# Attention backward: second half of dS transposed by DMA in eleven of fifteen steps of a head group instead of seven

## The chip, the cores and the metric

The kernel runs on one core of a Trainium2 chip. The metric is the device time of one execution in microseconds (us). The core has TensorE (PE; its weight loads are listed apart as PEld), VectorE (DVE), ScalarE (ACT), GpSimd (POOL), SyncE (SP), which here only issues DMAs, and 16 DMA engines that work through what SP and ACT issue. Each engine has its instructions in an order fixed by the program; between engines they wait on semaphores.

## The reference

The model is four layers on x of 2048 x 640: a linear attention (A), a sliding window attention (B), and both again with the same weights. The kernel computes the output and the gradients of the input and of the four weight matrices (`jax.vjp`). What the change touches is the backward of layer B, whose forward is, for 32 heads of width 20 and a causal window of 256:

```python
scores = jnp.einsum("bhqd,bhkd->bhqk", q, k) * (Dh ** -0.5)
mask = (idx[:, None] - idx[None, :] >= 0) & (idx[:, None] - idx[None, :] < W)
p = _softmax(jnp.where(mask[None, None], scores, -1e9), axis=-1)
o = jnp.einsum("bhqk,bhkd->bhqd", p, v)
```

Its backward needs, for each block of 128 queries and 128 keys inside the window, E = exp(scores), the product dP of the output's gradient with V, dS = dP * E, and from these dQ = dS K, dK = dS' Q and dV = E' dO (the softmax's sums and the row term of its backward are worked into dO and into the padding of each head from 20 to 32 columns beforehand). In the kernel scores and dS lie with the keys on the partitions. dK and dV can use them as they are; dQ needs dS turned, 128 x 128 block by block.

## The kernel before

The order of the program is: `forward` (all four layers, with what the backward needs saved to DRAM), `B_attn_bwd` for layer 3, a phase `bwd_phase` of dense work (weight gradients, layer norms, the linear attention of layer 2), `B_attn_bwd` for layer 1, and a last `bwd_phase`.

`B_attn_bwd` is a loop written out by hand: the order in which it calls the engines is the order of the program on each of them (`tc.manual_schedule`). The first loads of `bwd_phase`, though, stand on SP's queue between the last DMAs of `B_attn_bwd`.

The 32 heads are taken in G = 8 groups of four. A group has NB = 15 steps; a step n (0 to NS - 1 = 119) covers one block of 128 queries (t = n % 15 + 1) against its three key blocks (`blocks`). A step has two halves, h = 2n + p, of two heads each: p = 0 is the first head pair and p = 1 the second. For each half the loop does, in this order:

- `dve_ds(h)`, line 1575: VectorE multiplies dP (in PSUM, tile `pair`) by E into `ds_sb`.
- `mm_s(h + 3)` and `mm_dp(h + 2)`, line 1540: TensorE computes the scores of a half that comes three halves later (K and Q) and dP of one that comes two halves later (V and dO). Both write `pair`, of which PSUM holds three: the scores of a half go where the dS of three halves ago was read, and dP goes over the scores of its own half once the exponential has read them.
- `act_exp(h + 3)`, line 1560: ScalarE's exponential from `pair` to `e_sb`; GpSimd masks two of its blocks (lines 1564 and 1567).
- `turn(h)`, from line 1578: dS of the half is transposed, either by six matmuls with the identity into the one PSUM tile `dsT_ps` (line 1588), or, where the condition in line 1581 holds, by one DMA transpose on SP's queue from `ds_sb` straight to `dsT` in SBUF (`dma_t`, line 326).
- `copy_t`, line 1592: what lies in `dsT_ps` is copied to `dsT`: on ScalarE for first halves, on VectorE for second halves, the latter in the first half of the next step. Where `turn` used the DMA there is nothing to copy.
- `evac`, line 1613: VectorE moves a finished accumulator `dqvk_ps` to `dqkv`, once a step.
- `mm_acc`, lines 1604 and 1608: TensorE accumulates dQ, dK and dV of the block whose own step was three steps ago, two heads in each half; its dQ part reads the `dsT` of that step. In step 2 of a group two blocks are done, all four heads of the last block of the group before in the first half, and the first block of this group in the second.

PSUM is full: three `pair` of two banks, `dsT_ps`, and `dqvk_ps`. `dsT` has eight buffers, one for each half, `ds_sb` five and `e_sb` seven, one for each step.

At the start of steps 0, 2, 4, ... 12 one load of the next group's slabs is put on SP: first Q, K, V and dO by DMA transposes out of DRAM, then K, Q and dO plain. In the last group the weights of the next phase (`wq`) are loaded in their place. So all DMAs of this loop are issued by SP, in the order in which the loop comes to them.

Of the kernel before, what the change touches and what calls it, by code (L numbers as in the profile page):

```python
# [200 lines left out]
class Kern:  # L201
# [1298 lines left out]
    def B_attn_bwd(self, l, dqkv, slab0=None, first=None):  # L1500
        nc, tc, D, T, TT, H, G, DP = self.nc, self.tc, self.D, self.T, self.TT, self.H, self.G, self.DP
        ld, E, DS, PR, TPS, TSB, ACC = {}, {}, {}, {}, {}, {}, {}
        with ExitStack() as st:
# [15 lines left out]
            NB = TT - 1  # L1519
            NS = G * NB  # L1520
# [57 lines left out]
            def turn(h):  # L1578
                n, p = divmod(h, 2)
                t = TSB[h] = pe.tile([P, 2, 3, P], BF, name="dsT", bufs=8)  # L1580
                if p == 1 and n % NB % 2 == 1 and n < NS - 6:
                    self.dma_t(t.rearrange("p i j q -> p (i j) q"),
                               DS[n][:, 2 * p:2 * p + 2].rearrange("p i j q -> p (i j q)"))
                    return
                ps = TPS[h] = pps.tile([P, 2, 3, P], BF, name="dsT_ps")
                for i in range(2):
                    for j in range(3):
                        nc.tensor.transpose(ps[:, i, j, :], DS[n][:, 2 * p + i, j, :], self.ident)  # L1588
# [38 lines left out]
            with tc.manual_schedule(engines={mybir.EngineType.PE, mybir.EngineType.DVE, mybir.EngineType.SP,  # L1627
# [7 lines left out]
                for h in range(2 * (NS + 4)):  # L1635
                    n, p = divmod(h, 2)
                    here = n < NS
                    if here and not p:
                        if n % NB == 0:
                            todo = loads(n // NB + 1) if n // NB + 1 < G else next_weights()  # L1640
                        if n % NB % 2 == 0 and todo:
                            todo.pop(0)()
                    if here:
                        dve_ds(h)
                        mm_s(h + 3)
                        mm_dp(h + 2)
                        act_exp(h + 3)
                        turn(h)
                    if (h - 1) % 2:
                        copy_t(h - 1)  # L1650
                    for o in done:
                        evac(*o)
                    done = []
                    if not p:
                        copy_t(h)
                    units = outs.get(n, [])
                    if len(units) == 2:
                        units, heads = [units[p]], range(4)
                    else:
                        heads = (0, 1) if p == 0 else (2, 3)  # L1660
                    for o in units:
                        mm_acc(*o, heads)
                        if heads[-1] == 3:
                            done.append(o)
# [84 lines left out]
```

## Time and profile before

| | |
|---|---|
| median of 3 runs | 2271.16 us (2267.75 to 2272.58) |
| profiled execution | 2272.93 us, of which the span 2271.2 |
| granted TensorE clock, mean | 0.964 |
| attention backward of layer 3, all 120 steps | about 782 to 1104 us |
| attention backward of layer 1, all 120 steps | about 1548 to 1870 us |
| DMA transposes of dS in the whole run | 106 (53 in each attention backward) |

The span is the time from the first to the last instruction in the profile; the time of an execution is a little longer. "Busy" is the sum of an engine's instruction times; a matmul's time is long against the distance to the next one, since they are pipelined, so that distances between starts say more about TensorE than its busy time does. In a timeline a row gives the start, the time, the engine, the line, what is written and what is read, and the number of instructions that were merged; in brackets is idle time before it, with what ended it. A window row gives the busy time of each engine in that stretch.

### The profile page before, as it was taken

How to read it: one execution, taken by the hardware profiler on the slowest of the kernel's cores; microseconds unless marked ns; L12 is line 12 of the kernel's file. 1: busy time of each engine (PE TensorE's matmuls, PEld its weight loads, DVE VectorE, ACT ScalarE, POOL GpSimd, SP SyncE). 2: the span in 40 equal slices, each digit the busy share in tenths (PEclk: the TensorE clock that was granted, in tenths of full speed). 3: DMA queues.
4: the chain of work that ended last, by engine and by line, in shares of the span. 5: the costliest groups of instructions: out<-in, count | busy, mean ns of one | idle time of the engine just before them, and what ended most of it. 6: DMA issues, size and time to landing. Idle time of an engine off the chain costs nothing. (4 is left out here: it accounts for less than half of the span.)

```text
span 2271.2 us, 68393 instructions
## 1 busy us (share of the span) xinstructions
PE 2020.9 (89%) x28066; PEld 1415.0 (62%) x28066; DVE 1452.7 (64%) x2990; ACT 1195.5 (53%) x1981; POOL 883.0 (39%) x1850
## 2 busy tenths in 40 slices
PE   6878998869998798998799889998998988997899
PEld 4645666646666577777566567656777775665664
DVE  6656777567776389899534359606889984443551
ACT  4527777527787488888422123216888871110330
POOL 1015566416777355555222113204555541220110
PEclk9989999989999899999899999999999999998999
DMA  7469988599997576767787789845776768877964
GB/s 261 164 156 197 188 169 184 131 234 212 208 212 155 121 134 125 130 131 138 162 175 157 186 172 210 172 111 125 121 132 124 133 137 180 194 166 189 197 146 102
DMA packets 930059, 371.29 MB, mean 163 GB/s; under 512 B 810064, under 2 KB 910032, under 8 KB 929488
## 3 DMA queue, kind: packets, MB, share of 16 engines
q1 hardware_dynamic: 851968, 293.13, 63.8%
q10 hardware_dynamic: 77776, 73.79, 10.4%
q8 instruction: 219, 3.59, 0.7%
q14 instruction: 96, 0.79, 0.1%
HBM read 109.02 MB, written 112.07 MB: 97 GB/s over the span
## 5 line engine op out<-in xcount | busy, mean ns | idle before, releaser
L1575 DVE TENSOR_TENSOR ds_sb<-pair,e_sb 128x768 bf16<-128x768 f32 x480 | 436.3, 948 | 27.0 <-PE pair L1540 23.6
L1560 ACT ACTIVATE e_sb<-pair 128x768 bf16<-128x768 f32 x480 | 389.3, 812 | 116.8 <-PE pair L1540 111.2
L804 POOL TENSOR_SCALAR_AFFINE_SELECT e_sb<-e_sb 128x384 bf16<-128x384 bf16 (+1 forms) x512 | 199.7, 409 | 381.5 <-ACT e_sb L795 340.1
L795 ACT ACTIVATE e_sb<-s_ps 128x1152 bf16<-128x1152 f32 (+2 forms) x256 | 273.7, 1069 | 104.9 <-PE s_ps L791 79.1
L1058 PE MATMUL mm_ps<-wq,dqT 128*128 128x320 bf16 x1920 | 284.6, 303 | 20.5 <-DMA dqT<-dqkv 19.0
L1567 POOL TENSOR_SCALAR_AFFINE_SELECT e_sb<-e_sb 128x256 bf16<-128x256 bf16 x448 | 182.9, 408 | 267.9 <-ACT e_sb L1560 259.6
L1058 PEld LDWEIGHTS <-om 128*128 128x128 bf16 x1760 | 176.1, 100 | 165.4 <-DMA om<-o 13.0
L1229 POOL TENSOR_TENSOR gw<-w,gcar 128x640 f32<-128x640 f32 x64 | 89.5, 1398 | 477.5 <-ACT w L1226 456.7
L1058 PE MATMUL mm_ps<-dqkv,om 128*128 128x480 bf16 x1280 | 269.6, 368 | 0.0
L1058 PEld LDWEIGHTS <-dqT 128*128 128x128 bf16 x1920 | 186.4, 99 | 97.6 <-DMA dqT<-dqkv 23.2
L1564 POOL TENSOR_SCALAR_AFFINE_SELECT e_sb<-e_sb 128x256 bf16<-128x256 bf16 x512 | 207.5, 409 | 91.3 <-ACT e_sb L1560 90.0
L1211 ACT ACTIVATE dh<-mm_ps 128x320 f32<-128x320 f32 x128 | 56.0, 438 | 329.2 <-PE mm_ps L1058 279.3
L1588 PE MATMUL dsT_ps<-ident,ds_sb 128*128 128x128 bf16 x2244 | 193.3, 224 | 29.2 <-ACT dsT L1592 25.7
L1588 PEld LDWEIGHTS <-ds_sb 128*128 128x128 bf16 x2244 | 140.4, 99 | 92.5 <-issue 89.2
L1592 ACT COPY dsT<-dsT_ps 128x768 bf16<-128x768 bf16 x240 | 191.0, 796 | 11.6 <-PE dsT_ps L1588 5.3
L1604 PE MATMUL dqvk_ps<-Ksl,dsT 128*128 128x32 bf16 x2160 | 167.6, 178 | 4.8 <-DVE dqkv L1613 3.0
L1604 PEld LDWEIGHTS <-dsT 128*128 128x128 bf16 x2880 | 156.3, 97 | 24.1 <-issue 22.0
L439 PE MATMUL mm_ps<-Wqkv_B,hnTB 128*128 128x320 bf16 x960 | 169.0, 306 | 0.6 <-DVE qk_slab L683 0.3
L1608 PE MATMUL dqvk_ps<-Qsl,ds_sb 128*128 128x32 bf16 x2160 | 165.4, 177 | 0.0
L1608 PE MATMUL dqvk_ps<-dOsl,e_sb 128*128 128x32 bf16 x2160 | 165.3, 177 | 0.0
L1540 PE MATMUL pair<-KTg,QTg 32*128 32x384 bf16 (+2 forms) x768 | 122.4, 323 | 26.1 <-DVE ds_sb L1575 24.3
L1608 PEld LDWEIGHTS <-ds_sb 128*128 128x128 bf16 x2880 | 145.2, 96 | 0.0
(199 smaller groups left out, 3919.3 us busy)
## 6 DMA issues: line engine op xcount, KB each, us to landing
qkvp<-qk_slab SPq DMA_DIRECT2D x64, 256.0 KB, 3.4
hn<-hn SPq DMA_DIRECT2D x64, 160.0 KB, 2.8
om<-hn SPq DMA_DIRECT2D x20, 512.0 KB, 4.5
qkvp<-v_slab SPq DMA_DIRECT2D x32, 256.0 KB, 3.1
o<-o SPq DMA_DIRECT2D x48, 160.0 KB, 3.1
om<-o SPq DMA_DIRECT2D x15, 512.0 KB, 4.6
Ksl<-qkvp SPq DMA_DIRECT2D x12, 512.0 KB, 4.5
Qsl<-qkvp SPq DMA_DIRECT2D x12, 512.0 KB, 4.6
```

Source lines behind the costliest of these rows:

```text
L439: nc.tensor.matmul(ps.t[:, w0:w0 + width], lhsT=lhsT(), rhs=rhs(), start=start, stop=stop)
L795: op("ACT", av(3 * nkt * P), lambda: nc.scalar.activation(e.t[:, 0:3, 0:nkt, :], s3.t[:, :, 0:nkt * P].rearrange("p h (i q) -> p h i q", q=P),
L804: nc.gpsimd.affine_select(out=v, in_=v, compare_op=ALU.is_ge, fill=0.0, base=0, pattern=[[0, h1 - h0], [1, P]], channel_multiplier=-1)
L1058: nc.tensor.matmul(ps.t[:, w0:w0 + width], lhsT=lhsT(), rhs=rhs(), start=start, stop=stop)
L1560: nc.scalar.activation(e, PR[h][:, :, 0:3 * P].rearrange("p i (j q) -> p i j q", q=P), ACT.Exp, scale=self.c_att)
L1564: nc.gpsimd.affine_select(out=e[:, :, j, :], in_=e[:, :, j, :], compare_op=ALU.is_ge, fill=0.0, base=0, pattern=[[0, 2], [-1, P]], channel ...
L1567: nc.gpsimd.affine_select(out=e[:, :, j, :], in_=e[:, :, j, :], compare_op=ALU.is_ge, fill=0.0, base=-1, pattern=[[0, 2], [1, P]], channel ...
L1575: nc.vector.tensor_mul(DS[n][:, hs], PR.pop(h)[:, :, 0:3 * P].rearrange("p i (j q) -> p i j q", q=P), E[n][:, hs])
L1588: nc.tensor.transpose(ps[:, i, j, :], DS[n][:, 2 * p + i, j, :], self.ident)
L1592: (nc.vector.tensor_copy if h % 2 else nc.scalar.copy)(TSB[h], TPS.pop(h))
L1604: nc.tensor.matmul(a[:, 0, hh, :], lhsT=TSB[2 * n + hh // 2][:, hh % 2, j, :], rhs=ld[g]["K"][:, k, cs], start=(i == 0), stop=(i == len(dq ...
L1608: nc.tensor.matmul(a[:, 1 + x, hh, :], lhsT=src[n][:, hh, j, :], rhs=ld[g][rhs][:, q, cs], start=(i == 0), stop=(i == len(dkv) - 1))
```

## The change

In a head group, `turn` gives the second half of step n to the DMA when n % 15 is 1, 3, 5, 7, 9, 11 or 13 before the change, and when it is 1, 3, 5 or 7 to 14 after it. The last six steps of the run (n >= 114) use TensorE in both. Nothing else is edited.

```diff
             def turn(h):
                 n, p = divmod(h, 2)
                 t = TSB[h] = pe.tile([P, 2, 3, P], BF, name="dsT", bufs=8)
-                if p == 1 and n % NB % 2 == 1 and n < NS - 6:
+                if p == 1 and n % NB not in (0, 2, 4, 6) and n < NS - 6:
                     self.dma_t(t.rearrange("p i j q -> p (i j) q"),
                                DS[n][:, 2 * p:2 * p + 2].rearrange("p i j q -> p (i j q)"))
                     return
```

On TensorE the six matmuls and six weight loads of such a half go, on VectorE its copy; on SP one DMA transpose comes in, behind the load of that step where there is one (steps 8, 10 and 12) and ahead of the first load of the next group (step 14).

## The prediction

> **What bounds the kernel now.** First the page: its span and its busy shares.
>
> ```profile
> span 2271.2 us, 68393 instructions
> PE 2020.9 (89%) x28066; PEld 1415.0 (62%) x28066; DVE 1452.7 (64%) x2990; ACT 1195.5 (53%) x1981; POOL 883.0 (39%) x1850
> ...
> L1592 ACT COPY dsT<-dsT_ps 128x768 bf16<-128x768 bf16 x240 | 191.0, 796 | 11.6 <-PE dsT_ps L1588 5.3
> ```
>
> No engine is full over the span, and the change lies only in the two runs of the attention backward (about 782 to 1104 us and 1548 to 1870 us). There four engines work within a tenth of each other, so I went to the windows and the timeline of a stretch in the middle of a head group. I call a step D if the second half of its dS is transposed by DMA, P if by TensorE. ScalarE's copy of line 1592 runs once in each step, for the first half, and marks the steps. From copy to copy, step 6 (P) lasts from 839.57 to 842.37, and step 7 (D) to 844.85:
>
> ```profile
> 839.57:842.37 2.80, 2.57 (x70) 2.19 (x66) 2.38 (x5) 2.22 (x3) 1.54 (x4) 1.00 0.98 106
> 842.37:844.85 2.48, 2.22 (x49) 1.58 (x46) 2.36 (x4) 2.37 (x5) 1.54 (x4) 1.00 0.79 178
> 901.60:941.60 40.00, 36.02 (x808) 28.64 (x808) 36.10 (x55) 34.37 (x46) 23.06 (x60) 1.00 0.67 129
> 941.60:982.30 40.70, 36.93 (x809) 29.18 (x808) 36.23 (x55) 34.52 (x46) 23.05 (x60) 0.96 0.70 126
> ```
>
> The columns are the window, its length, busy us of PE, PEld, DVE, ACT and POOL, the granted clock, the DMA engines' busy share and GB/s. P costs 2.80, D 2.48; the third row is a whole head group, 40.0 us, the fourth one in which the clock fell once. Now what sets each. The timelines of ScalarE and of TensorE:
>
> ```profile
> 839.57 0.80 ACT L1592 COPY dsT<-dsT_ps 128x768 bf16<-128x768 bf16 x1
> 840.26 0.82 ACT L1560 ACTIVATE e_sb<-pair 128x768 bf16<-128x768 f32 x1
> 841.66 0.81 ACT L1560 ACTIVATE e_sb<-pair 128x768 bf16<-128x768 f32 x1 [0.58 <-PE pair L1540]
> 842.37 0.79 ACT L1592 COPY dsT<-dsT_ps 128x768 bf16<-128x768 bf16 x1
> 843.11 1.68 ACT L1560 ACTIVATE e_sb<-pair 128x768 bf16<-128x768 f32 x2
> 844.85 0.80 ACT L1592 COPY dsT<-dsT_ps 128x768 bf16<-128x768 bf16 x1
> ```
>
> ```profile
> 840.42 0.50 PE L1588 MATMUL dsT_ps<-ident,ds_sb 128*128 128x128 bf16 x6 [0.23 <-ACT dsT L1592]
> ...
> 841.29 0.33 PE L1540 MATMUL pair<-KTg,QTg 32*128 32x384 bf16 x2
> ...
> 841.56 0.51 PE L1588 MATMUL dsT_ps<-ident,ds_sb 128*128 128x128 bf16 x6
> ...
> 843.98 0.34 PE L1540 MATMUL pair<-VTg,dOTg 32*128 32x384 bf16 x2
> 844.25 0.51 PE L1588 MATMUL dsT_ps<-ident,ds_sb 128*128 128x128 bf16 x6
> ```
>
> In a P step the copy (839.57) must first empty the one dsT_ps buffer; then come the second half's transposes (840.42, +0.85), behind them on TensorE the accumulation and the scores of a later half (841.29, +0.87), its exponential (841.66, +0.37) and the next copy (842.37, +0.71): 2.80. In a D step that loop does not exist, and another sets the pace: copy (842.37), the next exponential behind it on ScalarE (843.11, +0.74), the dP product, which overwrites the pair that this exponential reads (843.98, +0.87), the next step's first transposes behind it (844.25, +0.27), and the next copy (844.85, +0.60): 2.48.
>
> **The change, part by part.** In a group, steps 8, 10, 12 and 14 go from P to D. The last group has only step 8 of these before n reaches 114. That is 7 x 4 + 1 = 29 in each attention backward, 58 in all.
>
> *Removed, for each:* six TensorE transposes with their weight loads (0.335 from the first start at 841.56 to the accumulation behind them), one VectorE copy out of dsT_ps (mean 557 ns by its group, 134 of them now, 76 after) and its place between two uses of dsT_ps. These are not added up as costs: they are why the loop of 2.80 vanishes. *Price:* the step falls back to the loop of 2.48, which has neither the removed transposes nor VectorE's copy in it. That is 0.32 us a conversion.
>
> No two D steps follow each other now, so what a row of them takes must be bounded. From below: ScalarE alone, at its shortest distances (copy to exponential 0.69 at 844.85, exponential to exponential 0.87, exponential to copy 0.71 at 841.66), needs 2.27; VectorE's evacuations before and behind the D step stand 2.25 apart (841.42 and 843.67). With 2.27 for all, a pair takes 4.54 against 5.28 now: 0.74 a conversion, 43 us. From above: a pair that stays at 5.28 gains nothing. I take 2.48, since the loop that shows it closes within one step (copy to next copy) and its five links stay in the same order on ScalarE and TensorE when the next step is D too; the ends that could free it, an earlier exponential or an earlier dP product, are both queued behind the copy.
>
> *Added, for each:* one DMA transpose of 128x768 bf16 on SP's queue:
>
> ```profile
> L326 SPq DMA_TRANSPOSE dsT<-ds_sb x106: 1210/1223/3567, 785.6 to 1852.1; - x106
> ...
> DMA to landing us min/median/max: 2.5/2.6/6.4
> ```
>
> Issuing takes SP 1.22. In steps 8 to 13 two of them and one plain slab load (0.59 at 844.02) stand on SP in two steps: 3.03 of 4.96 us. They are hidden by SP's idleness; what is queued behind them are prefetches of the next group's slabs, the first of which, QTg, moves back by at most one issue, 1.2, with a group of time in hand. The result is read by the accumulation three steps later. Step 7's is issued at 842.75; the second half's accumulation begins 0.65 behind the copy, so in step 10 at 843.02 + 3 x 2.48 = 850.5 in a row of D steps: 7.7 us for 2.6 of landing, 6.4 at the worst. Priced at nothing; without the cover a late one stalls TensorE, and with it the scores and every engine, by what it lacks. Step 14's is read earlier, in the first half of step 2 of the next group, after 2.48 + 2.80 and a first half: still over 5.5 us. The reuse of buffers adds no wait: dsT has eight for half steps, so the transpose takes the place of the one four steps back, whose reader ran a step ago.
>
> One place is tighter, the last group of each run, where SP also issues the next phase's loads. In the first run, step 112's transpose is issued at 1086.88 for 3.26, a weight load follows at 1090.19 for 0.58, and step 113's new one would go at 1090.8 and land between 1093.4 and 1097.2; step 116 read its dsT at 1097.35. In the second run it goes at 1856.3, lands between 1858.9 and 1862.7, and is wanted at 1861.6. I take nothing, at worst 2 us for both.
>
> *Sum:* 58 x 0.32 = 18.6 us less. The profiled execution took 2272.9 (its span 2271.2), so 2254.3; it stood 1.8 above the median of the three runs, 2271.2. On that median: 2252.6.
>
> **Rivals.** *VectorE's pace (2.25) or ScalarE's own (2.27) sets the D rows.* Then 43 us less, 2228. For it: VectorE does step at 2.25 behind every D step. Against: it catches up there, for it takes 3.02 in the next; the copy loop of 2.48 repeats to 0.01 us.
>
> *A new wait eats half.* For example the exponentials and dsT_ps drift into each other so that a D in a row costs 2.56, the mean of 2.48 and 2.64: 0.16 a conversion, 9 us, 2262. Nothing in the trace shows it, but nothing shows two D in a row either.
>
> *The SP queue cannot keep up (slower).* In the last group one transpose took 3.26 to issue with the queue full. If two transposes and a load need more than the 5.28 of a pair now, that is from 2.35 us an issue, the rows go by SP and PE waits for dsT. At 2.7: 5.99 a pair, 0.71 more than now, about 3.5 pairs in 14 groups, 35 us: 2306. Against: outside the last group the issue is 1.2 to 1.9 in the timeline even beside slab loads, and the DMA engines stand at 0.67 of their time over a group.
>
> *The clock falls more often.* The group at 0.96 took 40.7 against 40.0: 0.7 for one fall. A group gains 4 x 0.32 = 1.3, so two falls in each D row (20 us) undo it; three in each of 14 rows cost 14 x 0.8 = 11 net: 2282. Against: PE is busy 2.22 of 2.48 in the D step, 90%, and 2.57 of 2.80 in the P step, 92%, both at clock 1.00. The Trainium skill ("TensorE: Matmul & The Clock Gate", "A second HAM failure mode: psum-queue depth-cycling") says that short idles of TensorE between groups of matmuls can make the gate swing between half and full clock; by that rule the new row, all short idles, would be this rival. The trace so far disagrees: D and P steps with such idles (0.23 at 840.42) run at 1.00 for whole groups.
>
> That the edit does not reach the program is excluded: SP's order has two or three of these transposes between slab loads where it had one.
>
> **How the numbers follow.** Forecast 0.74 (2246 to 2259, for the median's own scatter of 2 to 3 us and the last groups' 2); VectorE's pace 0.04; half eaten 0.11, spread over 2258 to 2270; SP 0.06; clock 0.05. The range 2244 to 2265 holds the first and most of the third. A measurement here tells 0.2% (4.5 us) from no change. Below 2266.6: 0.74 + 0.04 + 0.06 = 0.84; within: 0.05 of the third; slower: 0.11.
>
> **What would show it.** Right: copy to copy 2.48 in each of steps 7 to 14, a group at 40.0 - 1.3 = 38.7, 76 VectorE copies of dsT, 348 fewer transposes on line 1588, no growth of waits for the DMA of dsT beyond the 3.9 us of now, clock near 0.96. Wrong: copies 2.3 or 2.6 apart in the rows; dsT landing later than 5 us; PE waiting for dsT inside a group; falls of the clock to 0.5 in the rows.

## Result and profile after

The changed kernel took 2248.1 us (median of 4 runs, 2245.6 to 2250.4) against 2270.4 before (2267.8 to 2272.6): the ratio is 0.9904 with a 95% interval of 0.9883 to 0.9925, 22 us less. A second series gave 0.9902 (0.9871 to 0.9934), 20 us less. The forecast was 18.6 less.

The page of the profiled execution (2245.6 us), with the rows that stood in the prediction:

```profile
span 2243.1 us, 67682 instructions
PE 2011.5 (90%) x27718; PEld 1387.0 (62%) x27718; DVE 1422.9 (63%) x2932; ACT 1194.9 (53%) x1981; POOL 879.7 (39%) x1850
...
L1592 ACT COPY dsT<-dsT_ps 128x768 bf16<-128x768 bf16 x240 | 191.2, 797 | 23.0 <-PE dsT_ps L1588 5.2
```

TensorE lost 348 matmuls and 348 weight loads and VectorE 58 copies, as counted. The busy shares tell nothing of the gain: PE's went up. The timeline of ScalarE does. Here are steps 8 and 9 of a group and the start of step 10 (step 7 begins at 839.05):

```profile
841.52 0.80 ACT L1592 COPY dsT<-dsT_ps 128x768 bf16<-128x768 bf16 x1
842.22 1.59 ACT L1560 ACTIVATE e_sb<-pair 128x768 bf16<-128x768 f32 x2
843.96 0.80 ACT L1592 COPY dsT<-dsT_ps 128x768 bf16<-128x768 bf16 x1
844.65 1.60 ACT L1560 ACTIVATE e_sb<-pair 128x768 bf16<-128x768 f32 x2
846.39 0.80 ACT L1592 COPY dsT<-dsT_ps 128x768 bf16<-128x768 bf16 x1
```

TensorE's timeline of step 8 shows the same two links that paced a D step before, the dP product and the transposes behind it:

```profile
843.09 0.34 PE L1540 MATMUL pair<-VTg,dOTg 32*128 32x384 bf16 x2
843.36 0.51 PE L1588 MATMUL dsT_ps<-ident,ds_sb 128*128 128x128 bf16 x6
```

From copy to copy 2.43: copy 841.52, exponential 842.22 (+0.70), dP product 843.09 (+0.87), transposes 843.36 (+0.27), next copy 843.96 (+0.60). Neither VectorE nor ScalarE is the pace by itself. ScalarE's idle time before its copy rose from 11.6 to 23.0 us in the page's row, and VectorE waits before each evacuation:

```profile
842.73 0.41 DVE L1613 TENSOR_TENSOR dqkv<-dqvk_ps,ckv 128x240 bf16<-128x240 f32 x1 [0.25 <-PE dqvk_ps L1608]
...
845.16 0.41 DVE L1613 TENSOR_TENSOR dqkv<-dqvk_ps,ckv 128x240 bf16<-128x240 f32 x1 [0.29 <-PE dqvk_ps L1608]
```

The distances of all 240 copies, read from the two traces, account for the whole. The first three rows hold for steps 0, 1 and 4 to 14 of an undisturbed group; step 2, in which two blocks are done, takes 3.05 and step 3 2.46 in both kernels. The last row goes from the first copy to the last.

| us, copy to copy | before | after |
|---|---|---|
| P step | 2.80 | 2.80 |
| D step behind a P step | 2.48 | 2.48 |
| D step behind a D step | - | 2.43 |
| head group, undisturbed | 39.98 | 38.38 |
| two groups in which the clock fell | 40.66, 40.67 | 38.37, 38.37 |
| 14 steps of the last group, layer 3 / layer 1 | 40.27 / 38.46 | 40.07 / 39.06 |
| attention backward, layer 3 / layer 1 | 321.9 / 319.9 | 309.8 / 308.5 |

Fourteen groups at 1.60 are 22.4, the two falls of the clock that are gone 1.4, the last groups together 0.4 back: 23.4 of the 23.5 us between the two attention backwards in these profiles. The spans of these two profiled executions differ by 28.1. The other 4.6 lie in phases that the edit leaves alone, and the medians differ by only 22.

What the change does to the transfers is seen in the view of the tile dsT. Its rows here are SP's issues (min/median/max in ns), the idle time until dsT landed and how often (PE and its weight loads are counted each, so that one wait stands twice), and the us from issue to landing:

```profile
L326 SPq DMA_TRANSPOSE dsT<-ds_sb x164: 1209/1302/3931, 783.9 to 1826.7; - x164
...
  DMA dsT<-ds_sb: 7.8, 6
...
DMA to landing us min/median/max: 2.5/4.0/7.1
```

SP's queue in steps 7 to 14 of a group:

```profile
839.44 1.22 SPq L326 DMA_TRANSPOSE dsT<-ds_sb  x1
840.70 0.59 SPq L1484 DMA_DIRECT2D Ksl<-qkvp  x1
841.69 3.60 SPq L326 DMA_TRANSPOSE dsT<-ds_sb  x2
845.34 0.89 SPq L1484 DMA_DIRECT2D Qsl<-qkvp  x1
846.50 3.82 SPq L326 DMA_TRANSPOSE dsT<-ds_sb  x2
850.37 1.52 SPq L1484 DMA_DIRECT2D dOsl<-dOpt  x1
851.99 5.88 SPq L326 DMA_TRANSPOSE dsT<-ds_sb  x3
```

A row with x2 or x3 also holds the time in which SP waits for dS between its issues. In the first of these, the two issues themselves take 1.69 and 1.21, where one took 1.22 before. What is slow is the transpose that stands right behind a plain slab load, in steps 8, 10 and 12: over groups 0 to 6 it lands 5.6 us after its issue in the median, against 4.0 in steps 9, 11 and 13. Before the change the median of all was 2.6; now it is 4.0.

The readers of these steps do not wait, since they come three steps later; the three waits that make up the 7.8 us all lie in the last groups. How near it comes was read from the trace, as the time from the landing of each dsT to its first reader in groups 0 to 6: before the change never under 3.6 us; after it 0.9, 0.4 and 0.5 at the least in steps 8, 10 and 12. The windows of such a stretch of steps before and after (columns as in the prediction) show the DMA engines' share going from 0.66 to 0.95:

```profile
842.00:861.60 19.60, 17.65 (x402) 13.87 (x400) 17.86 (x26) 17.41 (x24) 11.53 (x30) 1.00 0.66 141
```

```profile
839.05:858.56 19.51, 18.39 (x407) 13.23 (x404) 17.37 (x26) 18.41 (x26) 12.32 (x33) 1.00 0.95 164
```

### The profile page after: what moved, and what is told of

Its sections match the earlier page's. It is cut to its first block, busy times and chain, and to the rows that moved or that the text cites. A ratio compares the mean times of both kernels' runs of the same rounds, so it can differ in the third digit from the quotient of the medians.

```text
span 2243.1 us, 67682 instructions
## 1 busy us (share of the span) xinstructions
PE 2011.5 (90%) x27718; PEld 1387.0 (62%) x27718; DVE 1422.9 (63%) x2932; ACT 1194.9 (53%) x1981; POOL 879.7 (39%) x1850
## 5 line engine op out<-in xcount | busy, mean ns | idle before, releaser
L1588 PE MATMUL dsT_ps<-ident,ds_sb 128*128 128x128 bf16 x1896 | 163.7, 224 | 17.0 <-ACT dsT L1592 15.3
L1588 PEld LDWEIGHTS <-ds_sb 128*128 128x128 bf16 x1896 | 115.7, 99 | 71.4 <-issue 69.5
L1608 PEld LDWEIGHTS <-ds_sb 128*128 128x128 bf16 x2880 | 144.9, 96 | 0.0
L1608 PEld LDWEIGHTS <-e_sb 128*128 128x128 bf16 x2880 | 144.6, 96 | 0.0
```

The lines of the kernel that those rows point to most:

```text
L1608: nc.tensor.matmul(a[:, 1 + x, hh, :], lhsT=src[n][:, hh, j, :], rhs=ld[g][rhs][:, q, cs], start=(i == 0), stop=(i == len(dkv) - 1))
```

## Experiments

A converted step loses three things at once: TensorE's transposes, VectorE's copy, and the second use of dsT_ps. Three runs give them back: the first TensorE's time alone, the second most of VectorE's time alone, the third the second use of dsT_ps, which can't be had without TensorE's transposes. In them, steps 8, 10, 12 and 14 are edited, and the distances of the copies in a group are compared, since single runs scatter by several us.

**TensorE's time alone.**

```diff
-                    for i, (k, n, j) in enumerate(dq):
+                    for i, (k, n, j) in list(enumerate(dq)) * (3 if more else 1):
...
-                        mm_acc(*o, heads)
+                        mm_acc(*o, heads, p == 1 and n % NB in (8, 10, 12, 14) and n < NS - 6)
```

> In the four converted steps of a group the dQ matmuls of the second half are done three times (12 more, each with its weight load, about 0.30 us of TensorE; the last repetition starts the sum anew, so the result is the same). This gives TensorE its time back without dsT_ps and without VectorE's copy. Loop theory: VectorE's loop goes from 2.25 to 2.55 in every second step and stays 2.25 between, 2.40 on average, under the 2.43 of the copy loop: 0 to 0.12 a step, run 2248 to 2255. Rival, the gain was TensorE's time: 58 x 0.30 = 17 back, 2265.

A single run took 2257.2 us; an undisturbed group takes 38.66, 0.28 more than the 38.38 of the changed kernel, for 4 x 0.30 = 1.2 us of matmuls. ScalarE's copies stand 2.49 and 2.45 apart:

```profile
843.14 0.80 ACT L1592 COPY dsT<-dsT_ps 128x768 bf16<-128x768 bf16 x1
...
845.63 0.80 ACT L1592 COPY dsT<-dsT_ps 128x768 bf16<-128x768 bf16 x1
...
848.08 0.80 ACT L1592 COPY dsT<-dsT_ps 128x768 bf16<-128x768 bf16 x1
```

TensorE's time is worth 0.07 of the 0.40 a conversion: it was not the gain. (The run is above the 2248 to 2255 expected. Fourteen groups at 0.28 are 4 us of it; its profile also has two falls of the clock of 0.7 each, and a single run can't tell the rest.)

**VectorE's time alone.** The evacuation is done twice behind the converted steps, which gives 0.40 us back in the place where the copy took 0.47 (841.42 less 840.95 before the change).

```diff
+                for _ in range(times):
+                    nc.vector.tensor_mul(
...
-                        evac(*o)
+                        evac(*o, 2 if not p and (n - 1) % NB in (8, 10, 12, 14) and n - 1 < NS - 6 else 1)
```

> Behind each of the four converted steps of a group VectorE's evacuation of dqvk_ps is done twice (0.32 to 0.40 more on VectorE, in the place where the copy of dsT stood). Loop theory: as with the repeated matmuls, 2.25 and about 2.6 in turn, 2.43 on average: 0 to 0.15 a step, run 2248 to 2257. Rival, the gain was VectorE's copy: 58 x 0.36 = 21 back, 2269.

A single run took 2263.9; a group takes 39.03, 0.65 more. VectorE's doubled evacuation (the line has another number here) and the copies around it:

```profile
846.23 0.41 DVE L1615 TENSOR_TENSOR dqkv<-dqvk_ps,ckv 128x240 bf16<-128x240 f32 x1
846.56 1.81 DVE L1575 TENSOR_TENSOR ds_sb<-pair,e_sb 128x768 bf16<-128x768 f32 x2
848.62 0.85 DVE L1615 TENSOR_TENSOR dqkv<-dqvk_ps,ckv 128x240 bf16<-128x240 f32 x2 [0.25 <-PE dqvk_ps L1608]
```

```profile
847.41 0.80 ACT L1592 COPY dsT<-dsT_ps 128x768 bf16<-128x768 bf16 x1
...
849.84 0.80 ACT L1592 COPY dsT<-dsT_ps 128x768 bf16<-128x768 bf16 x1
...
852.49 0.80 ACT L1592 COPY dsT<-dsT_ps 128x768 bf16<-128x768 bf16 x1
```

The step with the extra work takes 2.65 and the next one 2.43. Here the first theory's expectation was too low: 2.65 is VectorE's loop of 2.25 with 0.40 more, as said, but the step behind it cannot make it up, because the copy loop holds it at 2.43. The total of 2264 was neither the 2248 to 2257 of one theory nor the 2269 of the other. So VectorE's time is not nothing: 0.65 a group is 0.16 of the 0.40 a conversion, and with the copy's 0.47 in place of 0.40 an estimate is 2.25 + 0.47 = 2.72. By that estimate the edit pays because it takes away both: the dsT_ps loop of 2.80, and the copy with which VectorE's loop would be the next bound, little below it.

**The second use of dsT_ps.** The converted steps transpose on TensorE as well, and nothing reads it.

```diff
+                    if n % NB not in (8, 10, 12, 14):
+                        return
+                    ps = pps.tile([P, 2, 3, P], BF, name="dsT_ps")
```

> In the four converted steps of a group the six TensorE transposes into dsT_ps are done beside the DMA transpose, and what they write is not read; VectorE's copy stays out. Loop theory: the transposes must again wait until ScalarE has emptied dsT_ps, the loop of 2.80 is back, a group at 40.0 and the run near 2268 to 2270, though VectorE has kept its gain. Rival, VectorE's copy was the gain: the run stays near 2248. Rival, TensorE's time: 2268 too, which the run with repeated matmuls tells apart.

2274.3 in a single run, and a group at 39.92: all of the 1.60 but 0.06 is gone, with VectorE's copy still left out. The timeline of ScalarE (its copy is line 1595 here), and from TensorE's the second half's transposes (line 1591 here):

```profile
841.42 0.79 ACT L1595 COPY dsT<-dsT_ps 128x768 bf16<-128x768 bf16 x1
...
843.90 0.80 ACT L1595 COPY dsT<-dsT_ps 128x768 bf16<-128x768 bf16 x1
...
846.00 0.81 ACT L1560 ACTIVATE e_sb<-pair 128x768 bf16<-128x768 f32 x1 [0.58 <-PE pair L1540]
846.70 0.79 ACT L1595 COPY dsT<-dsT_ps 128x768 bf16<-128x768 bf16 x1
```

```profile
844.75 0.50 PE L1591 MATMUL dsT_ps<-ident,ds_sb 128*128 128x128 bf16 x6 [0.23 <-ACT dsT L1595]
```

The converted step is back at 2.80, with ScalarE's wait of 0.58 for `pair` and TensorE's of 0.23 for the copy as before the change. TensorE's time alone did not do that (2.49 and 2.45), and VectorE's copy is not there, so it is the one dsT_ps buffer, which the second transposes must wait for.

**First halves instead of second halves.** If ScalarE were the bound, its copy would be the one to take away.

```diff
-                if p == 1 and n % NB not in (0, 2, 4, 6) and n < NS - 6:
+                if p == 0 and n % NB not in (0, 2, 4, 6) and n < NS - 6:
```

> The first half of dS goes to the DMA in the eleven steps in place of the second: ScalarE's copy (0.80 us) falls away there and VectorE's copy (0.56) comes back. Loop theory: without ScalarE's copy the copy loop is gone, and VectorE's loop with its copy is left: dS 0.95, scores, dP and transposes 0.32 to the first transpose, 0.54 to the copy, 0.48 to the evacuation, 0.32 to the next dS: 2.6 a step where second halves took 2.43. A group goes from 38.4 to between 39.3 and 40.0, the run to 2260 to 2270. Rival: ScalarE is the fullest engine of a converted step (18.4 of 19.5 us in the rows), so that taking its copy away brings steps below 2.43 and the run below 2248.

2269.5 in a single run, with the same number of DMA transposes. In a row of converted steps VectorE goes round without a gap, 2.61 a step (838.06, 840.67, 843.29), and a group takes 40.0:

```profile
840.67 0.56 DVE L1592 COPY dsT<-dsT_ps 128x768 bf16<-128x768 bf16 x1
841.15 0.40 DVE L1613 TENSOR_TENSOR dqkv<-dqvk_ps,ckv 128x240 bf16<-128x240 f32 x1
841.46 1.81 DVE L1575 TENSOR_TENSOR ds_sb<-pair,e_sb 128x768 bf16<-128x768 f32 x2
```

The loop theory gave 2.6. ScalarE, with its copy gone from these steps, now waits for `pair` twice in each (0.64 and 0.35); VectorE's loop with its copy in it is longer than the copy loop of ScalarE.

**How far it goes: all fifteen steps.**

```diff
-                if p == 1 and n % NB not in (0, 2, 4, 6) and n < NS - 6:
+                if p == 1 and n < NS - 6:
```

> The second half of dS goes to the DMA in all fifteen steps of a group (n < 114). Loop theory (a step whose second half goes by DMA is paced by copy, exponential, dP, transposes, copy: 2.43 us; one by TensorE 2.80): four more steps of a group at 2.43, three at 2.43 instead of 2.48, so a group goes from 38.38 to about 36.8 and the run from 2248 to about 2223. Rival, SP and the DMA engines: in steps 0 to 7 two transposes of dS (1.2 to 2.3 us of issue each) now stand beside a transposed slab load (1.9 to 4.1), together 4.3 to 8.7 for two steps of 4.86; dsT lands late, PE waits for it, a group stays at 38.4 or more and the run at 2248 or above.

Ratio 0.9992 (0.9969 to 1.0015): no gain is left that these runs can tell. The rival was right. Steps do run at 2.43 where dsT is in time, but in groups 1 to 6 SP starts the transposes of steps 6 to 9 some 3 us after their dS is ready, dsT lands 8.3 us after it in the median of steps 6 and 8, and its reader stands waiting there. The idle time until dsT (counted as above) rose from 7.8 to 52.5 us:

```profile
  DMA dsT<-ds_sb: 52.5, 67
```

And a second thing comes with it, in the windows up to and from a late dsT. Their rows are followed by TensorE's waits for dsT from 1640 to 1675 (total, times, longest); the longest is the one at 1654.2:

```profile
1640.00:1654.50 14.50, 13.15 (x294) 9.77 (x292) 12.81 (x19) 13.66 (x18) 8.45 (x23) 1.00 1.08 175
1654.60:1675.00 20.40, 19.90 (x321) 13.46 (x322) 14.14 (x21) 15.32 (x19) 9.81 (x27) 0.50 1.08 178
```

```profile
PEld L1604 <- DMA dsT<-ds_sb: 1.4, 2, 0.9
PE dqvk_ps L1604 <- DMA dsT<-ds_sb: 1.0, 2, 0.8
```

The granted clock drops to 0.50 during that wait and stays there for 20 us. The copies are then 3.07 apart, paced by TensorE:

```profile
1659.95 0.80 ACT L1592 COPY dsT<-dsT_ps 128x768 bf16<-128x768 bf16 x1 [0.41 <-PE dsT_ps L1588]
...
1663.02 0.80 ACT L1592 COPY dsT<-dsT_ps 128x768 bf16<-128x768 bf16 x1 [0.36 <-PE dsT_ps L1588]
```

Over the second attention backward the clock was 0.83. Leaving out those that begin in the first three steps of a backward, the two backwards of this trace have nine stretches at 0.50, of 3.4 to 27 us, and eight of them begin within 5 us after the start of a TensorE wait for dsT of 0.9 to 2.3 us. So the forecast's two slower rivals, SP's queue and the clock, come together here, and the turning point lies between eleven and fifteen steps. That the wait causes the fall is read from this order in time and was not tested by a run of its own.

**Is it SP's order or the DMA engines?** All fifteen, with the transposed slab loads no longer four in a row.

```diff
+                fs = [f for _, _, _, f in self.attn_slabs(l, g, (slab0, slab1)[g % 2], ld.setdefault(g, {}))]
+                return [fs[i] for i in (0, 1, 4, 2, 5, 3, 6)]
```

> All fifteen steps by DMA as in the earlier run, but the loads of the next group's slabs in another order (QT, KT, K, VT, Q, dOT, dO at steps 0, 2, ... 12), so that the transposed ones don't stand four in a row. If SP's queue is what is late (four transposed loads of 2.6 to 3.9 beside eight transposes of 1.2 in 19.5 us), the lag that grew to 3.7 us by step 6 is spread: PE waits for dsT in few groups, a group near 37 and the run at 2225 to 2245. If the DMA engines themselves are the limit (busy share 1.04 over the loop with fifteen), the order changes little: 2260 to 2275.

Ratio 0.9971 (0.9948 to 0.9994). The run lies in the range of the second theory, 2260 to 2275. Two groups reach 36.9, the number that the loops give for fifteen steps; the others stumble. The idle time until dsT fell from 52.5 to 37.0 us, but the intervals of the two ratios overlap, and they come from different chips, so no gain in time is shown for the order. Nor does the run tell SP's queue from the DMA engines: in groups 1 to 6 SP still starts the transposes late, by 3.3 us in the median of step 10, where the first order had its worst in step 6, by 3.7. Which of the two is the limit stays open.

**Thirteen steps.**

```diff
+                if p == 1 and n % NB not in (0, 4) and n < NS - 6:
```

> Second halves by DMA in thirteen of fifteen steps (all but 0 and 4). Loop theory alone: two more conversions of 0.37 and less, a group at 37.6 and the run near 2237. Theory of the used-up cover: dsT came 0.6 us ahead of its reader at the least with eleven steps and not at all with fifteen; with thirteen SP falls behind in steps 1 to 7 (two transposes and a slab load, 1.2 + 1.2 + 2.6 to 3.9 for 4.86) by about half as much, so that PE waits for dsT in some groups and the clock falls in a few: 2240 to 2262.

Ratio 0.9886 (0.9861 to 0.9912), 2244.4. Most groups take 37.7, one stumbles (40.3), and the last ones take 42.8 and 42.1. The interval overlaps that of the eleven steps (0.9904, 0.9883 to 0.9925): the two extra steps are seen in the groups, not in the time.

**The last group.** From step 109 on, TensorE turns both halves (`n < NS - 11`).

> As the changed kernel, but from step 109 on (n < NS - 11, the last eleven steps) TensorE transposes both halves: the transposes of steps 110, 112 and 113 leave SP's queue. They stand there behind the loads of the next phase, and PE waited for the first of them in both runs and for one more in the second. Theory: the steps of 4.0 to 4.5 us in the last group go to 2.80, the last group from about 40.1 and 39.1 to about 38.5 in both, 2 us of the run. Rival: those steps wait for something else at the end of the loop and stay.

The last groups go to 38.65 and 38.55, and no wait for dsT is left in the profile. So in the steps of 4.0 and 4.3 us there TensorE waited for a dsT whose transpose stood behind the next phase's loads. The kernel before had such a step too, of 4.38. A single run took 2240.8; the series of runs gave 0.9864 (0.9845 to 0.9882) on one chip, and beside the changed kernel on another:

> The eleven steps of the changed kernel, TensorE for both halves from step 109 on, timed. The last groups at 38.6 instead of 40.1 and 39.1 are 2 us; the one look was 2240.8. Theory: 2 to 3 us below the changed kernel, ratio to the kernel before 0.988 to 0.990 (the changed kernel has 0.9904, 0.9883 to 0.9925). Rival: the last steps were also worth what the first look showed, 7 us: 0.986.

> The changed kernel itself, beside the one that only leaves the last eleven steps to TensorE, on one chip. Its ratio to the kernel before again near 0.990. Theory (the late transposes of the last group cost what the profile shows, 2 us): the two lie 0.001 apart. Rival (they cost more, outside the loop): 0.003 or more.

> The eleven steps, TensorE for both halves from step 109 on, again, on the chip of the changed kernel. Theory: 0.001 under the changed kernel's ratio. Rival: 0.003 or more under it.

On that chip the changed kernel had 0.9902 (0.9871 to 0.9934) and this one 0.9907 (0.9877 to 0.9936): the two are the same as far as these runs resolve, and they don't resolve the 2 us of the profile. The first series, 0.9864, had met the rival's number, but beside the changed kernel the 7 us did not come again. One kernel with 0.9864 on one chip and 0.9907 on another also says how far ratios from different chips can be compared: not to 0.004.

**Both together**, thirteen steps and `n < NS - 11`:

> Thirteen of fifteen steps by DMA (all but 0 and 4), and TensorE for both halves from step 109 on. If the two effects are apart from each other: groups at 37.7 instead of 38.4 (seen with thirteen), the last groups at 38.6 instead of 42 to 43: about 13 x 0.65 = 8 us below the kernel that only takes the last steps out, 2230 to 2236 on the scale where the kernel before has 2272; ratio near 0.983. If a late dsT and a fall of the clock come in one group of thirteen, as they did once with thirteen steps (40.3 for 37.7), 2 to 5 us of that go.

Ratio 0.9847 (0.9823 to 0.9871), 2238.6 where the kernel before took 2273.0, a little above the 2230 to 2236 expected. In the profile groups 1 to 6 of both attention backwards take 37.7 each, no wait for dsT is left, and the two backwards take 304.5 and 304.6 us against 309.8 and 308.5 of the changed kernel. It has the lowest ratio of all runs, but on its chip the eleven steps with the same last group had 0.9864 (0.9845 to 0.9882), and the intervals overlap: that it is faster than those is not shown. Over about two of its groups the DMA engines' share is 1.03:

```profile
818.50:894.00 75.50, 69.93 (x1549) 52.23 (x1546) 66.92 (x97) 68.74 (x91) 46.17 (x121) 1.00 1.03 167
```

The run with fifteen steps stood at 1.08 in the windows around its late dsT. So a share of 1 is not where the waits begin: thirteen steps at 1.03 still had none.

## Why the prediction was right, and where it was off

*The two loops.* Right. The P step stayed at 2.80 and the D step went by copy, exponential, dP, transposes, copy. That the wait for dsT_ps makes the 2.80 is shown by the run that gives back its second use, and with it TensorE's transposes, but not VectorE's copy: 2.80 again. TensorE's time alone makes 2.49 and 2.45, most of VectorE's time alone 2.65. The prediction gave the removed work no price of its own. For TensorE's time that is nearly right, but VectorE's copy, had it stayed, would by the estimate above have been the next bound.

*The price, 0.32 a conversion.* Too small: 1.60 a group is 0.40. One link of the sum was mis-sized. Copy to exponential was put at 0.74, from a D step that follows a P step, where `pair` comes late; in a row it is 0.70, as it already was at 844.85 (0.69), a row that the prediction used for its lower bound. So a D step behind another takes 2.43: 4 x 0.37, and 0.05 for each of the three older D steps that now follow one, 1.63 for the 1.60 measured. Fourteen groups at 1.60 are 22.4; the medians differ by 22 in the first series and by 20 in the second.

*VectorE's and ScalarE's own pace (2.25, 2.27) as the bound of a row.* Fell: VectorE waits 0.25 to 0.29 in each step, and ScalarE's idle time before its copy went up. Half of the gain eaten: fell. (Over a group three engines, not four, lie within a tenth of each other: TensorE 36.02, VectorE 36.10 and ScalarE 34.37; the next, the weight loads, has 28.64.)

*The DMA transposes priced at nothing.* Right in time, off in the reason. The slack was put at 7.7 us against 2.6 of landing, 6.4 at the worst, a cover of at least 1.3. In groups 0 to 6 landing came up to 7.9 us after dS was ready: up to 2.0 of waiting on SP, and up to 6.7 from issue to landing, the most in the steps right behind a plain slab load. The cover was 0.4 at the least. Two marks that the prediction had named came out the other way: dsT landed later than 5 us, and the idle time until dsT grew from 3.9 to 7.8 instead of staying. The first had no cost, the second lies in the last groups.

*The last groups, nothing to 2 us.* Right: 0.2 less in the first, 0.6 more in the second, where a step that took 2.80 before now takes 4.00 because its dsT is late.

*SP's queue and the clock as slower rivals.* Not reached with eleven steps, both real with fifteen. Against SP's queue the prediction held issues of 1.2 to 1.9 outside the last group; the kernel before has one of 2.13 there, at 998.09. The clock's rival was weighed by TensorE's short idles alone. They did not do much: the D steps in a row ran at 1.00. But the kernel before has two falls, of 3.41 us each, at 949.63 and 1635.71, with no idle of TensorE over 0.4 us in the 6 us ahead of them, so short idles are not ruled out as a cause of a single fall. The long falls came with late transfers, which the prediction did not connect with the clock.

## What to carry to other kernels

Where several engines are each nearly full, don't price an instruction by its duration: find the loop of waits that closes from one step to the next, and ask which of its links the edit takes out and which loop is next (here 2.80, then 2.43; VectorE's was 2.25 without its copy and about 2.7 with it). The next loop's links should be measured from a step whose neighbours will be those of the changed kernel. And work moved to DMA is free only up to the slack of its reader: look at the least time from landing to reader, not at the median landing, before moving more.

## What the runs showed of the hardware that was not expected

With fifteen steps, one wait of 0.9 us for dsT came with 20 us at a granted clock of 0.50, in which PE was busy for 19.90 of 20.40 us by the profile. The Trainium skill ("TensorE: Matmul & The Clock Gate", "What's actually happening") has the clock return to full after about one busy window of 3.4 us. This trace disagrees with that for the profile's busy time: the stretch lasted 20.48 us, six such windows. What the gate counts as busy can't be seen here. In all traces of this case, every stretch at 0.50 between 700 and 1880 us is a whole multiple of 3.41 us long, from 3.41 to 27.31.

The time from issue to landing of the same 128x768 transpose went from 2.6 us in the median, with the DMA engines at a share of about 0.7, to 4.0 at 0.9, while the bytes moved in the attention backward grew only from about 133 to 155 GB/s. The slowest were those issued right behind a plain slab load (5.6 us in the median).
